# The fifteenth row group of w4 as sixteen transfers of 8, 1, 2, 3 … 15 rows

## The chip, the cores and the metric

The kernel runs on one core of a Trainium2 chip. The time is device microseconds of that core for one execution. The core has five engines that run their own instruction streams (PE for matmuls, with PEld for its weight loads; DVE and ACT for elementwise work; POOL; and SP, which here only issues transfers), and 16 DMA engines that carry the transfers.

## What is computed

Two branches read the same two rows `x` (batch 2, one position, 1024 wide) and are mixed by a gate:

```python
g = sigmoid((x * gate_w).sum(-1, keepdims=True))
# A: attention of one position against a cache of 16384 positions, 32 heads of 128
q = (x @ wq) per head
p = softmax(einsum("bhqd,bhkd->bhqk", q, k_cache) * 128 ** -0.5)
a = einsum("bhqk,bhkd->bhqd", p, v_cache) @ wo
# B: a small MLP mixer
h  = gelu(layernorm(x) @ w1)
x1 = x + shift(h) @ w2          # with one position the shifted h is all zeros
b  = x1 + gelu(layernorm(x1) @ w3) @ w4      # w3: 1024 x 3584, w4: 3584 x 1024
out = g * a + (1 - g) * b
```

All inputs are bf16. `k_cache` and `v_cache` are 268 MB each: nearly all of what is read.

## The kernel before

One large SBUF tile, `mem`, is cut into five cells of 32 KB for each of its 128 partitions. A unit of work is one pair of heads of one batch entry: 32 units. A unit's keys are one transfer of 128 rows of 64 KB (`load_k`, L109), into cells 0 and 1 or 1 and 2 by turns, and its values another (`load_v`, L114), into cells 3 and 4. All of these, and the weights, are issued by SP on one hardware queue, in program order; only w2 and three short rows of `x` and `gate_w` go by ACT's queue. DVE transposes keys (L418), PE forms the scores (L424), softmax runs on ACT and DVE (L442 to L472), PE multiplies with the values (`pv`, L474). A hardware loop (L666) runs 15 rounds of two units; `in_order` fixes the order on each engine as written.

The last unit (`last_unit`, L618) loads its values into cells 0 and 1, then starts on the weights of the output: `load_wo` (L548) takes wo, 8 MB, into cells 3 and 4, whose values `pv(0)` has read, and `load_w4` (L555) takes w4 in six pieces listed in `W4_PIECES` (L532). A piece is (cell, row group at which it stands there, first row group of w4, number of row groups, quarters of the output columns). w4's 3584 rows are laid over 128 partitions, so that partition p holds rows 28p to 28p+27; *row group* r is row 28p + r of all 128 partitions, 2 KB for each partition. Piece 0 (groups 0 to 14, 30 KB for each partition) goes to cell 2, which is free once the last keys are transposed, so it is issued right behind wo; the others go to cells 0 and 1 and are issued behind `pv(1)`, whose values lie there. The last two pieces are the two column halves of group 27.

`load_apart` (L543) issues one transfer from SP with a semaphore of its own (`tail_sems`), to which a finished transfer has added 16. `output` (L634) runs on PE once the last unit is done: the residual and the heads' results, then wo as soon as its semaphore is at 16, then each piece of w4 when its own semaphore is at 16 (L640). `add_rows` (L377) does four matmuls for each row group, one for each quarter of the columns (two in the halves). `write_out` (L567) copies finished column halves and stores them.

Of the kernel before, what the change touches and what calls it, by code (L numbers as in the profile page):

```python
# [23 lines left out]
def kernel(  # L24
# [15 lines left out]
    nc = tc.nc  # L40
    P = nc.NUM_PARTITIONS
# [20 lines left out]
    G1 = D // Q4  # L62
# [17 lines left out]
    def region(cell, elements, offset=0):  # L80
        at = cell * CELL + offset
        return mem[:, at : at + elements]
# [14 lines left out]
    rows = const.tile([B + 1, D], BF16, name="rows")  # L97
# [279 lines left out]
    def add_rows(actT, first, weight, quarters, last, group):  # L377
        wide = len(quarters) * G1
        n = weight.shape[1] // wide
        for r in range(n):  # L380
            for k, g in enumerate(quarters):
                mm = nc.tensor.matmul(  # L382
                    arows[g][QP * g : QP * g + B, :],
                    lhsT=actT[:, first + r, :],
                    rhs=weight[:, r * wide + k * G1 : r * wide + (k + 1) * G1],
                    start=False,
                    stop=(last and r == n - 1),
                    skip_group_check=True,
                )
                tc.declare_no_dep(mm.ins, group=group, reason="tail semaphores")  # L390
        return mm
# [3 lines left out]
    def mlp_residual():  # L395
        for r in range(KC):
            for g in range(Q4):
                nc.tensor.matmul(
                    arows[g][QP * g : QP * g + B, :].rearrange("b (i r) -> b r i", r=KC)[:, r, :],
                    lhsT=x1g[:, r, :],  # L400
                    rhs=ident_f[:, QP * g : QP * (g + 1)],
                    start=(r == 0),
                    stop=False,
                    skip_group_check=True,
                )
# [103 lines left out]
    def turn_heads():  # L509
        apart = mlp.tile([P, B, H, Q4], BF16, name="apart")  # L510
        for b in range(B):
            nc.vector.tensor_tensor(
                out=apart[:, b],
                in0=o_all[:, b].unsqueeze(2).to_broadcast([P, H, Q4]),
                in1=mask4[:].unsqueeze(1).to_broadcast([P, H, Q4]),
                op=ALU.mult,
            )
        ps = misc_psum([P, B, QP])
        for b in range(B):
            nc.tensor.matmul(  # L520
                ps[:, b], lhsT=apart[:, b].rearrange("p h c -> p (h c)"), rhs=lane_b[:],
                start=True, stop=True,
            )
        t = mlp.tile([P, QP, B], BF16, name="o_turned")
        nc.vector.tensor_copy(out=t[:], in_=ps[:].rearrange("p b r -> p r b"))
        return t
# [3 lines left out]

    ALL, LOW, HIGH = (0, 1, 2, 3), (0, 1), (2, 3)
    W4_PIECES = (  # L532
        (2, 0, 0, 15, ALL), (0, 0, 15, 7, ALL), (0, 7, 22, 3, ALL), (0, 10, 25, 2, ALL),
        (0, 12, 27, 1, LOW), (1, 0, 27, 1, HIGH),
    )
    tail_sems = [tc.alloc_semaphore(f"tail{k}") for k in range(1 + len(W4_PIECES))]
    wo = region(V_CELL, QP * D)


    def tail_group(k):  # L540
        return "tail_end" if k == len(W4_PIECES) else "tail"

    def load_apart(k, out, in_):  # L543
        dma = nc.sync.dma_start(out=out, in_=in_).then_inc(tail_sems[k], 16)
        tc.no_tile_sem_insts.add(dma.ins.name)
        tc.add_to_no_dep_group(tail_group(k), dma.ins)
# [4 lines left out]
    def w4_piece(k):  # L551
        cell, at, r, n, quarters = W4_PIECES[k]
        return region(cell, n * len(quarters) * G1, at * D)

    def load_w4(k):  # L555
        cell, at, r, n, quarters = W4_PIECES[k]
        src = B_w4.rearrange("(p r) n -> p (r n)", p=P)
        first = r * D + quarters[0] * G1
        load_apart(1 + k, w4_piece(k), src[:, first : first + n * len(quarters) * G1])


# [5 lines left out]
    def write_out(quarters):  # L567
        for g in quarters:
            at = out_row[:, g * G1 : (g + 1) * G1]
            row = arows[g][QP * g : QP * g + B, :]  # L570
            if g % 2 == 0:
                nc.vector.tensor_copy(out=at, in_=row)
            else:
                nc.scalar.activation(out=at, in_=row, func=ACTF.Copy)
        at = slice(quarters[0] * G1, (quarters[-1] + 1) * G1)
        dma = nc.sync.dma_start(out=out_rows[:, at], in_=out_row[:, at]).then_inc(stored, 16)
        tc.no_tile_sem_insts.add(dma.ins.name)
        tc.add_to_no_dep_group("stored", dma.ins)
# [39 lines left out]
    def last_unit(hp):  # L618
        V_LAST = 0
        score_first(hp, 1)  # L620
        load_v(hp, 1, V_LAST)
        score_second(1)
        softmax_a(1)
        pv(0)
        load_wo()
        load_w4(0)
        pv_end(hp, 0)
        softmax_b(1)
        pv(1, V_LAST)
        for k in range(1, len(W4_PIECES)):  # L630
            load_w4(k)
        pv_end(hp, 1)

    def output():  # L634
        mlp_residual()
        o_turned = turn_heads()
        nc.tensor.wait_ge(tail_sems[0], 16)
        add_rows(o_turned, 0, wo, ALL, False, tail_group(0))
        for k, (cell, at, r, n, quarters) in enumerate(W4_PIECES):
            nc.tensor.wait_ge(tail_sems[1 + k], 16)  # L640
            group = tail_group(1 + k)
            mm = add_rows(h2T, r, w4_piece(k), quarters, r + n == FC, group)
            if quarters != ALL:
                tc.declare_fence(mm.ins, group=group)
                write_out(quarters)
        mark = nc.gpsimd.memset(end_mark[:], 0.0)
        tc.declare_fence(mark.ins, group="stored")
        nc.gpsimd.wait_ge(stored, 2 * 16)
# [17 lines left out]
    with tc.For_i(0, HP - 1, 1, iteration_sync="reg_based") as i:  # L666
# [3 lines left out]
        with tc.If(i >= HP - 2):  # L670
# [3 lines left out]
            for load in loads:  # L674
                for ins in nc.cur_bb.bb.instructions:
                    tc.declare_no_dep(
                        load.ins, ins, across_iterations=True, reason="last round"
                    )
    output()
    in_order()  # L680

# [29 lines left out]
```

## Time and profile before

| | |
|---|---|
| Time, median of 3 runs | 1330.99 us (1330.96 to 1331.17) |
| Profiled execution: its own time | 1331.01 us |
| Profiled execution: span from first to last instruction | 1329.1 us |
| PE busy | 756.4 us, 57% |
| DVE busy | 649.2 us, 49% |
| Bytes read | 572.53 MB, 431 GB/s over the span |

The span is 1.9 us shorter than the execution's own time. Busy shares are averages over the whole span; which work sets the end is read from the chain of work that ended last. Besides its views by instruction, the trace holds a record for each DMA packet: start, length, bytes and queue, without the number of the DMA engine that carried it. A 128-row transfer leaves 128 data packets and 16 packets of 4 bytes, which are the semaphore's increments. A packet begins within some 4 ns of the recorded end of the packet before it on its engine, so the packets can be strung together into 16 streams.

### The profile page before, as it was taken

The numbers are of one execution on the slowest core, as the hardware profiler recorded it, in microseconds if no ns is written. First come the engines' busy times: TensorE is split into PE (matmuls) and PEld (weight loads), VectorE is DVE, ScalarE is ACT, GpSimd is POOL, SyncE is SP. The second block draws the span as 40 slices with busy tenths as digits, with TensorE's granted clock in tenths as the row PEclk, the third lists the DMA queues.
The fourth block names the chain that finished last, engine by engine and source line by source line (L and its number), as shares of the span: only waits on it lengthen the run. The fifth ranks groups of instructions, "written<-read, shape, count | busy, mean of one in ns | idle before, by whom it ended". The sixth has DMA issues, their size and how long they took to land.

```text
span 1329.1 us, 13066 instructions
## 1 busy us (share of the span) xinstructions
PE 756.4 (57%) x5000; PEld 330.9 (25%) x5000; DVE 649.2 (49%) x514; ACT 130.4 (10%) x204; POOL 12.2 (1%) x48
## 2 busy tenths in 40 slices
PE   1555566555556655555665555566555556655554
PEld 1222222222222222222222222222222222222222
DVE  1554455544445554444555544455554445555420
ACT  0011110011111001111100111110011111001110
POOL 1000000000000000000000000000000000000000
PEclk9777888777788877778887777888777788877776
DMA  9999999999999999999999999999999999999998
GB/s 410 439 440 419 433 440 438 424 432 440 436 428 432 440 428 432 436 440 428 430 438 440 422 434 440 436 426 432 440 430 434 432 440 428 432 436 440 426 432 355
DMA packets 10824, 572.69 MB, mean 431 GB/s; under 512 B 1207, under 2 KB 1467, under 8 KB 1726
## 3 DMA queue, kind: packets, MB, share of 16 engines
q1 hardware_dynamic: 10664, 570.43, 99.3%
q10 hardware_dynamic: 150, 2.10, 0.4%
q8 instruction: 8, 0.13, 0.0%
q14 instruction: 2, 0.02, 0.0%
HBM read 572.53 MB, written 0.00 MB: 431 GB/s over the span
## 4 chain that ended last, share of the span: by engine, by line
DMA 34%; PE 6%; DVE 6%; issue 6%; PEld 1%; DVEq 0%; ACT 0%; PEldq 0%; SPq 0%; ACTq 0%
DMA mem<-in_A_k_cache_dram 29%; DVE KT L418 6%; PE S L424 6%; DMA mem<-in_B_w_dram 2%; DMA mem<-in_A_v_cache_dram 2%; PE oacc L478 1%; PEld L424 0%; PEld misc L496 0%; DVEq L418 0%; ACT osb L491 0%; PEld misc L471 0%; PE arow L382 0%; SPq L110 0%; DVEq L706 0%; PEld misc L455 0%
## 5 line engine op out<-in xcount | busy, mean ns | idle before, releaser
L424 PE MATMUL S<-KT,qw 128*128 128x512 bf16 x2048 | 545.2, 416 | 361.2 <-DVE KT L418 361.1
L418 DVE STREAM_TRANSPOSE KT<-mem 128x2048 f32<-128x2048 f32 x256 | 570.6, 2282 | 265.3 <-DMA mem<-in_A_k_cache_dram 209.4
L424 PEld LDWEIGHTS <-qw 128*128 128x128 bf16 x2048 | 216.0, 105 | 681.9 <-issue 477.0
L478 PE MATMUL oacc<-mem,pt 128*8 128x512 bf16 x2048 | 118.4, 385 | 7.5 <-DMA mem<-in_A_v_cache_dram 7.5
L449 ACT ACTIVATE Dm<-ident_s,m 128x128 f32<-128x128 f32 x32 | 12.9, 402 | 971.1 <-PE oacc L478 942.4
L462 ACT ACTIVATE pt<-St,nb 64x256 bf16<-64x256 f32 x64 | 89.7, 1402 | 61.2 <-DVE nb L460 60.2
L500 DVE TENSOR_SCALAR o_all<-misc,g_rep 128x2 f32 (+1 forms) x32 | 7.0, 220 | 163.7 <-PE misc L496 163.7
L471 PE MATMUL misc<-rs,lmat 128*128 128x1 f32 x64 | 18.7, 362 | 107.9 <-ACT pt L462 61.2
L478 PEld LDWEIGHTS <-pt 128*8 128x8 bf16 x2048 | 47.2, 87 | 75.7 <-issue 23.9
L496 PE MATMUL misc<-lane,osb 128*128 128x2 f32 x256 | 33.8, 254 | 45.3 <-ACT osb L491 45.3
L472 DVE RECIPROCAL rinv<-misc 128x1 f32<-128x1 f32 x32 | 5.4, 168 | 108.5 <-PE misc L471 60.4
L445 DVE STREAM_TRANSPOSE St<-S 128x512 f32<-128x512 f32 x32 | 22.9, 717 | 66.3 <-PE L478 64.3
L496 PEld LDWEIGHTS misc<-lane,osb 128*128 128x128 f32 x256 | 31.5, 193 | 61.0 <-ACT osb L491 31.6
L471 PEld LDWEIGHTS misc<-rs,lmat 128*128 128x128 f32 x64 | 16.0, 310 | 114.5 <-ACT pt L462 64.9
L491 ACT ACTIVATE osb<-oacc,rinv 128x512 f32<-128x512 f32 x32 | 22.0, 687 | 88.5 <-PE oacc L478 88.5
L462 ACT ACTIVATION_READ_ACCUMULATOR pt<-St,nb 64x1 f32 x64 | 30.6, 477 | 0.0
L368 POOL TENSOR_TENSOR qw<-qdu,mask 128x16 bf16<-128x16 bf16 x32 | 7.4, 263 | 1150.5 <-PEq L670 1075.7
L460 DVE TENSOR_REDUCE nb<-misc 64x1 f32<-64x64 f32 x64 | 14.2, 222 | 6.7 <-PE misc L455 4.2
L455 PE MATMUL misc<-Dm,ones_f 128*128 128x128 f32 x64 | 16.3, 340 | 0.0
L447 DVE TENSOR_REDUCE m<-St 128x1 f32<-128x256 f32 x32 | 13.4, 420 | 1.1
L224 PE MATMUL misc<-ident_b,rows 3*128 3x3 bf16 x8 | 0.6, 197 | 22.6 <-DMA rows<-in_gate_w_dram 22.6
L455 PEld LDWEIGHTS misc<-Dm,ones_f 128*128 128x128 f32 x64 | 10.7, 210 | 0.4 <-issue 0.4
(94 smaller groups left out, 88.5 us busy)
## 6 DMA issues: line engine op xcount, KB each, us to landing
mem<-in_B_w_dram SPq DMA_DIRECT2D x1, 7168.0 KB, 27.5
mem<-in_B_w_dram SPq DMA_DIRECT2D x1, 3840.0 KB, 41.4
mem<-in_B_w_dram SPq DMA_DIRECT2D x1, 2048.0 KB, 12.2
mem<-in_B_w_dram ACTq DMA_DIRECT2D x1, 2048.0 KB, 12.4
mem<-in_B_w_dram SPq DMA_DIRECT2D x1, 1792.0 KB, 30.8
mem<-in_B_w_dram SPq DMA_DIRECT2D x1, 768.0 KB, 32.1
mem<-in_A_k_cache_dram SPq DMA_DIRECT2D x32, 27.9
mem<-in_A_v_cache_dram SPq DMA_DIRECT2D x32, 32.4
```

The source lines that it names most:

```text
L418: nc.vector.transpose(out=kt[:], in_=Kc.rearrange("p j d -> p (j d)").bitcast(FP32))
L424: nc.tensor.matmul(S, lhsT=qw[b][:, v, NG - 1 - m : NG - 1 - m + P], rhs=ktb[:, half * GT : (half + 1) * GT, w, :, e], start=(first and n ...
L445: nc.vector.transpose(out=st[:].rearrange("p j r -> p (j r)"), in_=S[:])
L447: nc.vector.tensor_reduce(out=m[:], in_=st[:, :, 0:NG], axis=AX.XY, op=ALU.max)
L449: nc.scalar.activation(out=Dm[:], in_=ident_s[:], func=ACTF.Copy, scale=m[:, 0:1])
L455: nc.tensor.matmul(R_ps[:], lhsT=ones_f[:], rhs=Dm[:], start=True, stop=True)
L460: nc.vector.tensor_reduce(out=nb[rows], in_=R_ps[rows, rows], axis=AX.X, op=ALU.min)
L462: nc.scalar.activation(out=pts[b][rows, :, e, :].rearrange("p (m a) k -> p a k m", a=GT // 4), in_=st[rows, :, 0:NG].rearrange("p (a k) m ...
L471: nc.tensor.matmul(tot_ps[:], lhsT=lmat[:], rhs=rs[:], start=True, stop=True)
L478: nc.tensor.matmul(oacc[b][QP * q : QP * q + 8, :], lhsT=pts[b][:, g].rearrange("p h k -> p (h k)"), rhs=V[:, 4 * g : 4 * g + 4, :].rearra ...
L491: nc.scalar.activation(out=osb[:], in_=oacc[b][:], func=ACTF.Copy, scale=rinvs[b][:, 0:1])
L496: nc.tensor.matmul(ot[:], lhsT=osb[:, k * Dh : (k + 1) * Dh], rhs=lane[:, k : k + 5 : 4], start=(k == 0), stop=(k == 3),)
```

## The change

Piece 0 is cut in two. Its first 14 row groups stay one transfer of 128 rows (28 KB each). Row group 14 becomes a piece of its own, in the same place of the same cell: it is loaded by 16 transfers, each of some consecutive partitions: 8, then 1, 2, 3 and so on to 15 of them, 128 in all, 2 KB for each partition. All sixteen add to one semaphore, and PE waits until that is at 256.

```diff
     W4_PIECES = (
-        (2, 0, 0, 15, ALL), (0, 0, 15, 7, ALL), (0, 7, 22, 3, ALL), (0, 10, 25, 2, ALL),
-        (0, 12, 27, 1, LOW), (1, 0, 27, 1, HIGH),
+        (2, 0, 0, 14, ALL), (2, 14, 14, 1, ALL), (0, 0, 15, 7, ALL), (0, 7, 22, 3, ALL),
+        (0, 10, 25, 2, ALL), (0, 12, 27, 1, LOW), (1, 0, 27, 1, HIGH),
     )
+
+    STEPPED, STEPS = 1, (8, 1, 2, 3, 4, 5, 6, 7, 8, 9, 10, 11, 12, 13, 14, 15)
...
         first = r * D + quarters[0] * G1
+        if k == STEPPED:
+            assert sum(STEPS) == P
+            p = 0
+            for rows in STEPS:
+                load_apart(
+                    1 + k, w4_piece(k)[p : p + rows],
+                    src[p : p + rows, first : first + n * len(quarters) * G1],
+                )
+                p += rows
+            return
         load_apart(1 + k, w4_piece(k), src[:, first : first + n * len(quarters) * G1])
...
-            nc.tensor.wait_ge(tail_sems[1 + k], 16)
+            nc.tensor.wait_ge(tail_sems[1 + k], 16 * (len(STEPS) if k == STEPPED else 1))
```

`last_unit` issues pieces 1 and up in a loop behind `pv(1)` in its text. SP's stream in the changed kernel is: wo, piece 0 (14 groups), the sixteen short transfers with no wait of their own, and then the piece of seven groups, which is the first that waits for `pv(1)`. PE's, DVE's, ACT's and POOL's streams are the same instructions in the same order as before.

## The prediction

> **What bounds the kernel now.** I read the queues first.
>
> ```profile
> DMA  9999999999999999999999999999999999999998
> ...
> q1 hardware_dynamic: 10664, 570.43, 99.3%
> q10 hardware_dynamic: 150, 2.10, 0.4%
> q8 instruction: 8, 0.13, 0.0%
> ```
>
> Columns: packets, MB, share of 16 DMA engines. The engines are busy in every slice: transfers bound the kernel, so what counts at the end is when the last DMA engine is through with its last packet. Next, the chain that ended last, its last part in order of time (start, length, what):
>
> ```profile
> 1289.28 2.94 PE oacc L478 x21
> 1292.22 32.91 DMA mem<-in_B_w_dram
> 1325.17 0.38 PE arow L382 x2
> 1325.55 0.21 PE arow L382 x2
> 1325.77 0.25 PE arow L382 x2
> 1326.01 0.40 DVE out_row L572
> ```
>
> The tail is one wait for w4; behind it come few matmuls and the store. Third, SP's timeline:
>
> ```profile
> 1275.87 0.34 SPq L544 DMA_DIRECT2D mem<-in_A_wo_dram  x1
> 1276.33 17.31 SPq L544 DMA_DIRECT2D mem<-in_B_w_dram  x6
> ```
>
> By the single issues, piece 0 goes out at 1276.33 and the five others between 1292.22 and 1293.64, behind pv(1): SP is idle for 15.5 us between. Last, PE's weight loads in the tail (the bracket is the idle time before, and what ended it):
>
> ```profile
> 1317.75 2.62 PEld L382 LDWEIGHTS <-h2T 128*2 128x2 bf16 x60 [2.20 <-DMA mem<-in_B_w_dram]
> ...
> 1322.03 0.64 PEld L382 LDWEIGHTS <-h2T 128*2 128x2 bf16 x28 [1.66 <-DMA mem<-in_B_w_dram]
> ```
>
> PE waits for each piece of w4 and is done with it before the next has landed.
>
> **Streams of the 16 engines.** The packet records, strung together, show that the engines are not level. They finish their last piece at 1323.33, .46, .55, .78, .86, .94, 1324.41, .46, .84, .93, 1325.07, .20, .25, .27, .36 and .37: mean 1324.50, slowest 1325.37, so perfect levelling would gain 0.87 us. The spread is old: it stands at 2.09 us at 1287 too. It comes from the eight 16 KB instruction packets in the queue table. Five come by 165 us and three between 1304 and 1320, each on a different engine, and that engine is then 1.0 to 1.5 us later than it was.
>
> How a short transfer is spread is in the packet counts. q10 carried w2 (128 rows), x (2 rows) and gate_w (1 row): 128+16, 2+2 and 1+1 data and semaphore packets are its 150. q1: 74 transfers of 128 rows make 74 × 144 = 10656, and two stores of 2 rows, at 2+2 each, give 10664. So n rows use n engines here, one row each. The gate_w packet ran on one of the two engines that x used, which speaks for a fixed first engine. [...]
>
> **The change, part by part.** Engine e (0 to 15) then carries as many rows of group 14 as there are steps longer than e: 16, 15, 14, 13, 12, 11, 10, 9, 7, 6, 5, 4, 3, 2, 1, 0, in place of 8 each.
>
> *Row removed from a packet.* Packets of 30720 and 14336 bytes take 1.138 and 0.535 us (medians): 0.0368 ns a byte, so 2 KB off eight packets saves each engine 8 × 0.0754 = 0.60 us.
>
> *Row in a packet of its own.* The three 2048-byte packets of q10 took 0.084 us each; the next packet starts some 0.003 before the recorded end; each transfer adds a semaphore packet, 0.009 less 0.003. Together 0.0865 us a row. Engine 0: 16 × 0.0865 − 0.60 = +0.78 us; engine 7: +0.18; engine 8: 0.00; engine 15: −0.60; mean +0.09.
>
> *The end.* Strung back to 14 us, the two engines of x are those that end at 1323.46 and .55. With +0.70 and +0.78 they stay over 1 us ahead of the slowest: free. What decides is the number of the five that end between 1325.20 and 1325.37, which no record shows: if they are 11 to 15 they gain 0.26 to 0.60 and others at 1325.07 or a level engine 8 end it, some 0.3 earlier; if one is engine 2, it ends 0.61 later. Five among the numbers 2 to 15 leave the worst of them somewhat late on average. I take +0.2 us, bounds −0.3 and +0.6.
>
> *Issue on SP.* Sixteen more, each by the L544 rows (0.33 to 0.37 us): 5.9 us, from 1276.7 to 1282.6, inside the 15.5 us before pv(1) lets piece 2 go. The cover lasts up to 0.97 us each; past that the later pieces slip, but their data start only at 1315, 21 us after their issue, so the end moves only if an issue takes over 2 us. Zero.
>
> *PE's wait on 256.* One more wait, with piece 2's matmuls queued behind it. The 14 groups land 0.60 earlier, so their 56 matmuls (60 take 3.1 us now) run from about 1317.15 to 1320.1; group 14 lands by 1317.25 + 0.6 and is seen 0.5 later (as 1317.25 to 1317.75 now), 1318.4. Its four follow at once, and piece 2 starts at 1322.03 anyhow. Zero; without that cover, four matmuls, 0.2 us.
>
> Sum: span 1329.1 + 0.2 = 1329.3, execution 1331.01 + 0.2 = 1331.2; the median of the runs is 0.02 below that execution, so **1331.2 us**, bounds 1330.7 to 1331.6.
>
> **Rivals.**
>
> *It levels the engines (faster).* For: late streams owe it to instruction packets, which hit eight different engines and not the two that x used. Should these be 8 to 15, the ramp relieves just them, engine 8 by nothing; a gain of 0.1 to 0.5, 1330.7. Against: the slowest may be on the wrong side of 8. Even the best case, 0.87, gives 1330.1.
>
> *The landing side is shared (slower).* Short transfers put a row on engine j whatever partition it is for, so it can land beside rows that another engine streams to the same place. If a landing place takes only one engine's rate (65536 bytes in 2.42 us, 27 GB/s), a row costs both about 0.0754 more: engine e then changes by n × 0.162 (its relief is eaten by the rows of others), +1.1 for a late engine 8, +2.3 for a late engine 2, and with three at one place +3.3: 1332.1 to 1334.3. It decides once a late engine with n of 7 or more is delayed. Against: the packet of x's second row went out at 14.51 while the other engine had a 64 KB packet in flight (12.22 to 14.63), and both had plain lengths, 0.084 and 2.418. [...]
>
> *The queue or the engine balks at many transfers (slower).* No more than 7 of q1's transfers are in flight in this trace (wo and six pieces at 1293.6); here it is 23. If fewer are allowed, SP stalls until short ones have landed, near 1318, and the next piece begins late by landing to issue to first packet (the stores: issue 1326.50, first packet 1327.26), about 1 us: 1332. If the allowance is just 7, the steps themselves come at SP's 0.34 in place of 0.09, another 4: 1336. A pause behind each semaphore is the same in effect: the last two pieces follow each other in 0.345 us of eight packets without one, so it is at most 0.26 a step, 4.2 on engine 0, less its 1.0 of slack: 1334. [...]
>
> *It doesn't do what it says.* If each step begins at another engine, the ramp is gone and the mean of +0.09 is left: 1331.1.
>
> **How the numbers follow.** Forecast 0.61; levelling 0.12; shared landing 0.12; balking 0.06; no ramp 0.05; a drift between sessions, either way, 0.04. Within 0.2% (2.66 us, about what a measurement of this kernel can tell from no change) lie the forecast, levelling, no ramp, three quarters of shared landing and half of balking: 0.61 + 0.12 + 0.05 + 0.09 + 0.03 = 0.90. Slower: the rest of these two and half of the drift, 0.08. Faster: the other half of the drift, 0.02, since no case of the change reaches so far. The forecast's own range is 1330.7 to 1331.6; with levelling below and the lower half of shared landing and balking above it is 1330.3 to 1332.8, which leaves out some 0.13.
>
> **What would show it.** Right: sixteen transfers of 2 to 30 KB issued by 1283; q1 with 10664 + 128 rows + (8 + 1 + … + 15 = 128) semaphore packets = 10920; 2048-byte packets at 0.084; the ends of the streams moved by −0.6 to +0.8; PE not waiting for group 14. Wrong: 2048-byte packets of 0.15 us or more, or packets beside them stretched (shared landing); gaps in a stream (balking); issues after 1292; an end over 1 us away from 1325.4.

## The result and the profile after

The changed kernel takes 1336.04 us (median of 6 runs, 1335.41 to 1336.88) against 1331.05 us (1330.96 to 1331.41): ratio 1.0037, interval 1.0027 to 1.0047, 5.0 us slower. The forecast was 1331.2 us, range 1330.3 to 1332.8. The profiled execution took 1335.41 us, its span is 1333.5 us: 4.4 us more than before, and the lines below are from it.

The queues show as many packets on the main queue as the prediction counted for sixteen short transfers, 10920 (which engine carried which row, this count doesn't say):

```profile
span 1333.5 us, 13082 instructions
...
q1 hardware_dynamic: 10920, 570.43, 99.0%
```

The chain that ended last is another one. In order of time, from the first instruction of the output on (start, length, what):

```profile
1313.73 0.22 PE S L398 x2
...
1314.65 6.31 issue
1320.97 0.21 PE arow L398
```

and its end:

```profile
1330.22 0.10 PE arow L382 x2
...
1330.38 0.41 DVE out_row L584
```

Before, the tail was one wait of 32.91 us for w4, and the last matmuls followed the last landing. Now no transfer is left in it: it begins with PE at 1313.73, where before PE was at this instruction at 1298.62, and from there on it is PE's own work and one large gap. What PE waited for stands in the table of waits (engine and line, releaser, us in total, times, longest):

```profile
PE S L398 <- PEq L718: 16.6, 1, 16.6
DVE apart L512 <- PEq L718: 16.3, 1, 16.3
```

In the profile of before the same two waits are short:

```profile
PE S L398 <- PEq L706: 1.2, 1, 1.2
DVE apart L512 <- PEq L706: 0.9, 1, 0.9
```

L718 (L706 before) is the line that opens the kernel's context; the engines' meeting at the loop's exit is booked on it. In the trace's records of these sequencer instructions ACT, PE and DVE report there at 1295.81, 1296.73 and 1297.79, SP only at 1313.23, and all are let go at 1313.62. SP's timeline shows what kept it:

```profile
1291.26 21.00 SPq L546 DMA_DIRECT2D mem<-in_B_w_dram  x5
1330.88 0.70 SPq L588 DMA_DIRECT2D out_dram<-out_row  x2
```

Five issues that took 2.4 us before (1291.24 to 1293.64) take 21.0. By their single records three are plain (0.33 to 0.36 us); the fourth, the lower columns of group 27, begins at 1292.83 and takes 2.07 us; the fifth, the upper columns, begins at 1295.02 and takes 17.23 us, to 1312.25. SP stands in the instruction all that time, and the output begins 1.5 us after its end.

PE has slack in the tail, so 15.1 us of delay become 4.4. The table by stretches shows where it went (stretch and its length; busy us and number of instructions of PE, PEld, DVE, ACT, POOL; granted clock, DMA share, GB/s):

```profile
1298.00:1313.70 15.70, 0.00 (x0) 0.00 (x0) 0.00 (x0) 0.00 (x0) 0.01 (x1) 0.57 0.97 418
1313.70:1321.00 7.30, 0.95 (x58) 0.81 (x60) 0.49 (x2) 0.00 (x0) 0.08 (x1) 0.50 0.99 342
1321.00:1326.40 5.40, 5.08 (x128) 3.43 (x127) 0.23 (x1) 0.00 (x0) 0.00 (x0) 0.71 0.82 326
1326.40:1330.40 4.00, 3.44 (x120) 2.73 (x119) 0.02 (x1) 0.00 (x0) 0.00 (x0) 1.00 0.03 8
```

PE is idle to 1313.7. Then there is a gap of 6.31 us, as there was before in the same place (7.14 us), which the profile calls issue. It fits a wait for instructions: a 16 KB instruction packet ends at 1319.55 and the next matmul begins at 1320.97, and in all ten traces PE goes on 1.4 to 1.6 us after the end of such a packet. Only then does it do all of wo and w4, in 9.4 us, with one more gap of 0.56 us at 1326.44, which again ends 1.45 us after the end of an instruction packet (1325.54); no matmul in these 9.4 us waits for a transfer. The last row of w4 landed at 1326.98.

That landing is itself 1.6 us later than before (1325.37), and the second stretch shows it: the DMA engines are busy for 0.99 of it and move 342 GB/s, where 0.93 gave 398 GB/s between 1306 and 1317 before:

```profile
1306.00:1317.00 11.00, 7.24 (x135) 4.39 (x134) 0.23 (x1) 0.00 (x0) 0.00 (x0) 0.61 0.93 398
```

In the packet records the 128 packets of 2 KB take 0.084 us at the least and 0.158 at the most, mean 0.109; the 14336-byte packets beside and behind them average 0.628 us in place of 0.543. The stretching comes to all engines at once: between 1315.3 and 1318.6 there are 3.05 us in which at least fifteen of the packets in flight, one on each engine, are more than 5% longer than the shortest of their size; before, it is never more than five. So two things happened, neither of which was in the sum.

### The profile page after: what moved, and what is told of

The parts are those of the page before. It is cut to its first block, busy times and chain, and to the rows that moved or that the text cites. A ratio compares the mean times of both kernels' runs of the same rounds, so it can differ in the third digit from the quotient of the medians.

```text
span 1333.5 us, 13082 instructions
## 1 busy us (share of the span) xinstructions
PE 753.4 (56%) x5000; PEld 330.3 (25%) x5000; DVE 649.7 (49%) x514; ACT 130.4 (10%) x204; POOL 12.0 (1%) x48
## 3 DMA queue, kind: packets, MB, share of 16 engines
q1 hardware_dynamic: 10920, 570.43, 99.0%
```

## The experiments

Times are medians, with the kernel before run beside them on the same chip: 1331.13 us (25 runs) for the first four and 1331.09 us (25 runs) for the others. *Entries* are data and semaphore packets of SP's queue that one DMA engine has to carry: a 128-row transfer, 128 + 16 packets on 16 streams, puts 9 on each engine. The expectations call an engine's list of them a ring and suppose that its room is limited. No record of a trace gives such a limit; the runs test it. Counting from wo, before has 9 × 7 = 63 at the last issue; the steps make it 9 × 7 + 32 = 95 on engine 0.

**Row group 14 in one transfer.**

```diff
-    STEPPED, STEPS = 1, (8, 1, 2, 3, 4, 5, 6, 7, 8, 9, 10, 11, 12, 13, 14, 15)
+    STEPPED, STEPS = 1, (128,)
```

> Row group 14 stays a piece of its own with a wait of its own, but is loaded by one transfer of 128 rows. Ring theory (SP is held at its last two issues because the fullest engine's ring has no room, all engines leave the loop together, so PE starts the output 15 us late): no issue of SP over 0.4 us, PE in the output from about 1299, time 1331.1 as before. Shared-landing theory (2 KB rows land beside another engine's stream and stretch the transfers): also 1331.1. If the cut into 14 and 1 or PE's extra wait itself costs, 1333 or more.

1331.18 us (1331.02 to 1331.22, 10 runs), ratio 1.0000 (0.9991 to 1.0010). The last issue takes 0.37 us with 72 entries, PE starts the output at 1298.3, the 2 KB packets take 0.084 us (mean 0.0845). The cut and the added wait (on 16 here) cost nothing; all of the 5 us lies in the sixteen transfers.

**The last two pieces issued behind the loop.** The steps stay as they are.

```diff
-        for k in range(1, len(W4_PIECES)):
+        for k in range(1, len(W4_PIECES) - 2):
             load_w4(k)
...
     def output():
+        for k in range(len(W4_PIECES) - 2, len(W4_PIECES)):
+            load_w4(k)
         mlp_residual()
```

> The sixteen steps stay; the last two pieces of w4 are issued by SP behind the loop instead of in it. Ring theory: SP may be held at them up to about 1312, but nobody waits for SP there, so PE starts the output at about 1299 again and DMA ends the kernel: 1331 to 1332.5 (the DMA stream itself ended 1.6 us later in the changed kernel). Shared-landing theory (the slow rows set the end): 1335.5 to 1336.5 as in the changed kernel.

1332.77 us (1332.45 to 1333.09, 10 runs), ratio 1.0012 (1.0002 to 1.0022): 3.3 us below the changed kernel. First SP, then PE, in this kernel's timeline:

```profile
1299.26 13.21 SPq L546 DMA_DIRECT2D mem<-in_B_w_dram  x2
```

```profile
1299.30 0.22 PE L398 MATMUL S<-ident_f,x1g 128*2 128x32 f32 x2 [1.16 <-PEq L720]
```

SP is held as before, to 1312.5, and PE starts all the same. The end is a wait for DMA again (`DMA mem<-in_B_w_dram` to 1326.84). So the held issue costs what it costs through the loop's exit. What is left, 1.6 us, is the later end of the transfers (last row at 1327.03). The upper end of the expectation, 1332.5, was a little low.

**Eight transfers of 16 rows.**

```diff
-    STEPPED, STEPS = 1, (8, 1, 2, 3, 4, 5, 6, 7, 8, 9, 10, 11, 12, 13, 14, 15)
+    STEPPED, STEPS = 1, (16,) * 8
```

> Row group 14 by 8 transfers of 16 rows: 8 x 2 = 16 entries (data and semaphore) on each engine where the steps put 32 on engine 0; 15 transfers in flight in place of 23. Ring theory: entries on the fullest engine at the last issue 9 + 9 + 16 + 5 x 9 = 79 in place of 95, the last two issues are not held or by under 1 us, 1331.1. If it is the number of transfers in flight and 15 is too many: held, 1334 or more. Shared-landing theory: rows still land beside other engines' streams, 128 of them as before, so 1334 or more.

1332.26 us (1332.03 to 1332.72, 10 runs), ratio 1.0008 (0.9999 to 1.0018). The time expected by the ring theory was missed: with 79 entries the last issue is held after all, for 2.65 us to 1295.9, though PE still starts at 1297.7 and waits for DMA at the end. So the 1.1 us are the transfers' later end: 2 KB packets take 0.108 us in the mean, up to 0.172. This is the shared-landing theory's sign, without a held issue that delays PE, and a smaller size than it was given.

**Four transfers of 128 rows by 512 bytes.**

```diff
-    STEPPED, STEPS = 1, (8, 1, 2, 3, 4, 5, 6, 7, 8, 9, 10, 11, 12, 13, 14, 15)
+    STEPPED, STEPS = 1, (0, 1, 2, 3)
...
-            p = 0
-            for rows in STEPS:
+            for g in STEPS:
                 load_apart(
-                    1 + k, w4_piece(k)[p : p + rows],
-                    src[p : p + rows, first : first + n * len(quarters) * G1],
+                    1 + k, w4_piece(k)[:, g * G1 : (g + 1) * G1],
+                    src[:, first + g * G1 : first + (g + 1) * G1],
                 )
-                p += rows
```

> Row group 14 by 4 transfers of 128 rows of 512 bytes, one for each quarter of the columns: only 11 transfers in flight, each row on the engine that always serves it, but 4 x 9 = 36 entries on every engine, 99 in all at the last issue. Ring theory: the last issue of SP is held until 17 or 18 entries of the slowest engine are done, near 1315 to 1317, PE starts the output at 1316 to 1318, time 1336 to 1340. Theory of a limit on transfers in flight, and shared-landing theory: 1331.1 to 1331.5, no issue held.

1336.85 us (1335.98 to 1337.74, 4 runs), ratio 1.0043 (1.0026 to 1.0060). Only 11 transfers are in flight here, and SP is held as never before: three issues in a row, the last two in this line (to 1314.11).

```profile
1296.00 18.11 SPq L546 DMA_DIRECT2D mem<-in_B_w_dram  x2
```

PE starts at 1316.0. The last issue was done a little before the expected 1315. The 512-byte packets take 0.027 us throughout (largest 0.041), and the last row lands at 1325.67, 0.3 later than before. So a limit on the number of transfers falls, and so does shared landing as the sole cause: this kernel has the held issue almost alone, and is as slow as the changed one. The sum of entries over all engines doesn't set the hold either: it is 1152 with the one transfer, which wasn't held, and 1136 in the two kernels with additional transfers below, which were.

**Eleven transfers of 11 rows and one of 7.**

```diff
+    STEPPED, STEPS = 1, (11,) * 11 + (7,)
```

> Row group 14 by 11 transfers of 11 rows and one of 7: 12 transfers, 24 entries on engines 0 to 6, 87 in all at the last issue (95 with the steps, 79 with 8 transfers of 16 rows, where the last issue was held until 1295.9). Ring theory: the last issue is held longer than in that run and shorter than with the steps (1312.3), to between 1297 and 1306, and PE starts the output some 1.4 us behind that; PE still catches up with the transfers, so the time is that of the stretched DMA streams, 1331.8 to 1333. If the held issue did not matter in itself, PE would start at 1299 whatever SP does.

1332.84 us (1332.66 to 1333.47, 10 runs), ratio 1.0013 (1.0004 to 1.0023). The last issue is held to 1308.63 and PE starts at 1310.12: between the neighbours, but later than the 1306 expected. The time is as expected; a start at 1310.1 is still early enough for PE to catch up with the stretched streams, and a wait for DMA ends the chain again.

**Sixteen transfers of 8 rows.**

```diff
+    STEPPED, STEPS = 1, (8,) * 16
```

> Row group 14 by 16 transfers of 8 rows: engines 0 to 7 get 32 entries each, as many as engine 0 with the steps, engines 8 to 15 none. Ring theory: the last issue is held as long as with the steps or up to 2 us longer, since engine 5, which is 2 us late, now has 32 entries too: until 1312 to 1314.5, PE starts at 1313.5 to 1316, time 1335.5 to 1338. If the staircase itself (uneven engines) were the cause, the time would differ by more than that.

1337.44 us (1336.27 to 1337.89, 4 runs), ratio 1.0046 (1.0029 to 1.0063). Held to 1313.66, PE from 1315.14. The ramp is not needed for the loss: 32 entries on engines 0 to 7 do the same.

**Eight additional transfers of 8 rows, in two layouts.** Both kernels are the one before with 64 rows of 2 KB more, loaded into unused space behind piece 0. They differ in the lines below: a transfer takes eight neighbouring partitions (minus) or every fourth one (plus). The author assumed that in steps of 4 each row lands where its engine also lands the rows of a 128-row transfer, and in a block most do not. That is not shown: no record says which engine carries which partition.

```diff
         for t in range(8):
-            rows = slice(8 * t, 8 * t + 8)
+            first = 32 * (t // 4) + t % 4
+            rows = slice(first, first + 29, 4)
             load_apart(EXTRA, spare[rows], src[rows])
```

> The kernel before, with 8 additional transfers of 8 rows (2 KB each) behind piece 0, a copy of half of row group 14 into 2 KB of cell 2 that nothing reads; PE waits for them behind piece 0. [...] Shared-landing theory: packets of 0.084 us; engines 0 to 7 carry 8 x 0.0865 = 0.69 us more; time 1331.1 to 1331.8. Theory that short transfers as such are slow (a pause or a stretch per transfer): packets of 0.12 to 0.14 us as in the changed kernel, 1332 to 1333.

> [...] Shared-landing theory: packets of 0.12 to 0.14 us, streams beside them stretched, time 0.4 us or more above the run with steps of 4. Theory that short transfers as such are slow: the same packets and the same time as with steps of 4, within 0.2 us.

Steps of 4: 1331.87 us (1331.71 to 1332.06, 10 runs), ratio 1.0006 (0.9996 to 1.0015). Rows in a block: 1332.66 us (1332.38 to 1332.95, 10 runs), ratio 1.0012 (1.0002 to 1.0021). The ranges of ten runs don't touch. With steps of 4 all 64 packets take 0.084 to 0.086 us and the 14336-byte packets 0.555 in the mean; in a block the 2 KB packets go up to 0.142 and the 14336-byte packets average 0.611. Same number of transfers, same bytes, same partitions in all: the 0.8 us come from which rows go together in a transfer. (The layout with steps of 4 is 0.8 us over before, a shade more than expected, for 0.69 us of additional work on eight engines. In both, 79 entries held the last issue for 2.2 to 2.4 us, with no effect on PE.)

So the theory's effect is there, but not in the theory's form. The packets are shorter than it expected: 35 of the 64 in a block are as short as with steps of 4. And the stretching isn't kept to the engines with additional rows. By the spread that the prediction counted, one row on each engine, eight rows use eight engines. Yet with rows in a block there are 2.9 us, from 1316.2 to 1319.1, in which at least fifteen packets in flight, one on each engine, are over 5% longer than the shortest of their size. So packets of engines that carry no additional row are stretched too. The changed kernel and the others that load row group 14 in blocks of partitions show 3.0 to 3.5 us of this each; before, with one transfer, with four and with steps of 4 there are never more than 11 stretched packets at once. Between the two layouts a transfer's rows differ in w4 as they do in `mem`, so the pair doesn't tell the writing side from the reading side. What ties the engines together stays open.

| entries on the fullest engine | kernel | last issue done | PE starts the output | time |
|---|---|---|---|---|
| 63 | before | 1293.6 | 1298.6 | 1331.05 |
| 72 | one transfer | 1293.6 | 1298.3 | 1331.18 |
| 79 | 8 × 16 rows | 1295.9 | 1297.7 | 1332.26 |
| 87 | 11 × 11 rows and 7 | 1308.6 | 1310.1 | 1332.84 |
| 95 | steps (the change) | 1312.3 | 1313.7 | 1336.04 |
| 95 | 16 × 8 rows | 1313.7 | 1315.1 | 1337.44 |
| 99 | 4 × 128 rows | 1314.1 | 1316.0 | 1336.85 |

## Why the prediction was wrong

**Issue on SP, costed at zero: this step failed.** The sixteen short issues were indeed done by 1282.1 and cost nothing. But the step went on to say that later issues only matter if their data are late, and that needed over 2 us an issue. Two later issues took 2.07 and 17.23 us, and even so no data were late. What the step did not ask is who else waits for SP: the last two issues stand in the loop's body, and no engine leaves the loop before SP does (SP reports at 1313.23, the others are let go at 1313.62). The wait in the profile of before that could have told it is the 1.2 us of PE on PEq L706, right ahead of the output. The delay of PE costs 3.3 of the 5.0 us, by the kernel that issues the last two pieces behind the loop. (The step also misread the single issues: the first of the five others went out at 1291.24 and not at 1292.22, so SP was idle for some 14.5 us and not 15.5. And 1.138 and 0.535 us are the shortest packets of their sizes, not the medians, 1.140 and 0.539. Neither changes the forecast.)

**"The queue balks at many transfers" was the right suspicion, at 0.06, with the wrong limit and the wrong way to the end.** It counted transfers (7 seen, 23 to come). Four transfers of 128 rows, 11 in flight, were held longer than anything else; what the holds go by is entries on the fullest engine: in the table the last issue is done at 1293.6 with 72, at 1295.9 with 79, at 1308.6 with 87 and at 1312.3 or later with 95 and 99. And it let the loss come from data that start late, by 1 us or by 5; the transfers never ran dry (0.97 and 0.99 busy in the first two stretches). Its 1336 agrees with the result by accident.

**Shared landing was right that it matters which partitions a short transfer takes, and belonged in the sum; its mechanism is not shown.** The two layouts show the effect: 0.084 to 0.086 us with steps of 4, up to 0.142 in a block, and up to 0.158 in the changed kernel. The row that spoke against it, one 2 KB packet of x at its plain length (0.084 us) beside a 64 KB packet, was a single one. The term "0.0865 us a row" held only for undisturbed rows; the mean was 0.109 us for the packet alone. Most of the loss lies in the long packets: over the shortest of their size, those of 14 KB lose 0.74 us on each engine (before: 0.06) and those of 28 KB 0.27, against 0.20 in the 2 KB ones. The rival charged the engine that brings a row and the one whose place it is; the traces show at least fifteen stretched at once, with the block layout also engines that carry no additional row. Which engine serves which place, no record shows. The measured price, 1.1 to 1.8 us in the kernels where PE doesn't set the end, lies at the bottom of the range given (1332.1 to 1334.3), but was not reached by the rival's way.

In the changed kernel the two losses don't add: PE's late start almost alone (the four transfers of 512 bytes, where it is 2.3 us later still) costs 5.7 us, the stretched transfers alone 1.1 to 1.8, both together 5.0, because PE is still at work when the late rows land.

**The spread of short transfers held**: besides the count of 10920, the packets can be strung into sixteen streams that carry 16, 15, 14 … 9, 7 … 1 and 0 of the 2 KB packets. They also give, for the changed kernel, what was left open, which numbers the late engines have, since a stream shows its number by its count of 2 KB packets: the five that are 1.8 to 2.1 us behind the first when they begin w4 carry 11, 4, 3, 2 and 1, so they are engines 5, 11, 12, 13 and 14. By the plain arithmetic four of the five would have been relieved by 0.26 to 0.52 us and engine 5 burdened by 0.35. But all streams were stretched, the one without a 2 KB packet too, and the last ended later, not earlier: it is engine 5's, at 1326.97.

**PE's wait on 256** cost nothing by itself, as forecast: PE came to it after the rows had landed, and the additional wait of the kernel with one transfer was free.

That the hold goes by entries of the fullest engine is shown by order, not by one number: at the moments when held issues got free, I count 77 to 85 entries on the fullest engine whose packets had not ended. What holds the issue, and whether the count is of something close to entries, stays open.

## What to carry to other kernels

When an edit adds transfers, count what each of the 16 DMA engines then has outstanding, not the transfers or their bytes, and look at what stands behind the issuing engine: here the last issue, with 95 entries on the fullest engine, held SP for 17.23 us, and at the loop's exit PE, DVE and ACT waited for SP until 1313.62. Keep an issue that may be held out of the loop's last round (1332.77 us in place of 1336.04), or load the same bytes in few long transfers (one of 128 rows: 72 entries, 0.37 us for the last issue). Here the packets fit a spread of one row on each engine, from the same first engine on; rows in blocks of neighbouring partitions stretched at least fifteen packets at once for some 3 us, while rows in steps of four partitions stretched five at a time at the most.

## What the runs showed of the hardware that was not expected

An issue of 128 rows takes 0.33 to 0.43 us, one of a single row 0.23 us, one of two rows 0.25, of fifteen 0.38: among the steps of 1 to 15 rows the time grows, by and large, with the engines it goes to. Eight rows of neighbouring partitions take 0.28 to 0.37 us, eight in steps of four partitions 0.62 to 0.80. A held issue is an instruction that lasts longer (17.23 us, and 20.41 with 16 transfers of 8 rows); the table of waits doesn't list it, only the timeline shows it.

PE's gap of 6 to 7 us behind the loop is in both kernels: PE stops at 1314.65, the 16 KB packet begins at 1318.56. On its stream it follows directly behind long packets, so it seems to have waited its turn; when it was asked for, no record shows. With this gap PE needs 16.7 us from the start of the output to its last matmul, of which the kernel before hides all but the last few matmuls.
